# Turning q by a transposing DMA in a pooled attention feeding a GELU layer, with matmuls on zeros and a later load in the first batch

## The chip, the cores and the metric

The kernel runs on one core of a Trainium2 chip. The metric is device time in microseconds (us), the median of several executions. Five engines work side by side, each in the order of its own queue, and wait for each other through semaphores: TensorE (PE; its weight loads are listed as PEld), VectorE (DVE), ScalarE (ACT), GpSimd (POOL) and SyncE (SP). SP, ACT and POOL also issue DMAs. SBUF is the on-chip memory of 128 partitions, PSUM the eight banks that TensorE writes.

## The reference

Inputs are q, k and v of 8 batches, 8 heads, 576 positions and 64 values, and two weight matrices of 512 x 2048 and 2048 x 512, all float32.

```python
k_p = k.reshape(B, H, Sp, 8, D).mean(axis=3)      # Sp = 72
v_p = v.reshape(B, H, Sp, 8, D).mean(axis=3)
scores = scale * np.matmul(q, k_p.transpose(0, 1, 3, 2))
attn = softmax(scores)
attn_out = np.matmul(attn, v_p)                   # (B, H, S, D)
x = attn_out.transpose(0, 2, 1, 3).reshape(B * S, H * D)   # 4608 x 512
g = gelu_tanh(x @ w_in)                           # 4608 x 2048
return g @ w_out                                  # 4608 x 512
```

## The kernel before

The work is written out by hand in one order for every engine; no planner moves it. After a start for batch 0 there are nine stages g = 0 to 8. Stage g runs the two dense layers on rows 512g to 512g + 511 of x, and beside them the attention of batch nb = g + 1, as far as there is one.

A stage has two halves. In the first, TensorE does 64 matmuls of the first layer (`p1_mm`, L266: four per group `fo`, 128 x 512 each), and ACT applies GELU to each group (L272). Between groups the kernel puts work for the next batch, in the lists of `plan`: adding k over its eight pooled positions and v likewise (L135, on VectorE), transposing k (`trans_k`, L162) and q (`trans_q`, L179). A transpose is a TensorE matmul against an identity into a PSUM bank, and VectorE (in batch 0 also ACT) copies the result to `qT` (L184, L186). In the second half TensorE does 64 matmuls of the second layer (`p2_mm`, L275), and at nine fixed places among them the attention of the next batch: scores (`qk`, L196), exponentials (`expo`, L202, ACT), the product with v (`av`, L215; L220 for batch 0), the logarithm and exponential that give the reciprocal of the sum (`norm`, L228 to L233, ACT), and the multiply that writes x transposed, `xT` (`mult`, L241, VectorE). The last multiplies of a batch come behind the last store copy of the stage (L280), and the next stage's first layer reads what they write. TensorE works strictly in its queue's order, so a score matmul that waits holds everything behind it.

In batch 0 the eight score pairs and then eight steps of product, norm and multiply run ahead of stage 0, with 16 first-layer matmuls on 288 columns among the last three steps. In stage 0 the plan has v at groups 1 and 2, k at 7, q at 8 to 11 and the transposes of k at 13.

Loads of k, q (cast to bfloat16) and v of batch g + 2, and the weights, are issued from POOL, and each waits until its buffer is free; two buffers of q alternate. k and v of batch 0 and v of batch 1 are issued from SP at the very start (L76, L96), k's second half from ACT. All stores of the output are issued from SP (L286), from six output buffers.

In `qT` the columns of a head are in the order of positions: `qT[.., h, c, t]`, where q's rows were loaded with 32 groups of 18 positions, c is the group and t one of nine pairs. The two positions of a pair lie on the two halves of the partitions, and `kT` is padded with zeros so that each half can be scored alone.

Of the kernel before, what the change touches and what calls it, by code (L numbers as in the profile page):

```python
# [8 lines left out]
F32 = mybir.dt.float32  # L9
BF16 = mybir.dt.bfloat16  # L10
ALU = mybir.AluOpType
# [7 lines left out]
def kernel(  # L19
# [9 lines left out]
    nc = tc.nc  # L29
    B, H, S, D = q.shape  # L30
    Sp = S // 8
# [6 lines left out]
    TP = T // 2  # L38
    CH = S // 2
# [8 lines left out]
    consts = ctx.enter_context(tc.tile_pool(name="consts", bufs=1))  # L48
    kvp = ctx.enter_context(tc.tile_pool(name="kvp", bufs=2))
    qp = ctx.enter_context(tc.tile_pool(name="qp", bufs=2))  # L50
    bp = ctx.enter_context(tc.tile_pool(name="bp", bufs=2))
# [7 lines left out]
    PS = psp.tile([128, 8, 512], F32, name="PS")  # L59


    vs, qs = {}, {}
# [10 lines left out]
    def load_v(b, eng, h0=0, h1=H):  # L73
        if b not in vs:
            vs[b] = kvp.tile([Sp, H, 512], F32, name="vt")
        eng.dma_start(out=vs[b][:, h0:h1],  # L76
                      in_=v[b, h0:h1].rearrange("h (j l) d -> j h (l d)", l=8))
# [15 lines left out]
    load_k(0, [nc.sync, nc.scalar])  # L93
    load_v(0, nc.sync, 0, 4)
    load_v(0, nc.sync, 4, 8)
    load_v(1, nc.sync)  # L96
    load_q(0, 0, 1)
    load_q(0, 1, 2)
    make_identity(nc, identb)
# [4 lines left out]
    xT = consts.tile([128, KO, N], BF16, name="xT")  # L104

    kTs = [consts.tile([128, 2, H, Sp], BF16, name=f"kT{i}") for i in range(2)]
# [3 lines left out]

    vz = consts.tile([Sp, PR, 2, 2, D], BF16, name="vz")
    ones = consts.tile([Sp, 2, 2, D], BF16, name="ones")
    nc.vector.memset(kts[0][0:64, KR], 0.0)
    nc.vector.memset(kps[0], 0.0)
    nc.vector.memset(kTs[0], 0.0)
# [16 lines left out]
    qTs = {}  # L132
# [22 lines left out]
    def half_bank(bank):  # L155
        return PS[:, bank, :].bitcast(BF16)

    def trans_k(b, bank, odd_eng=None):
        tp = half_bank(bank)[:, 0:(KR + 1) * 128].rearrange("p (r c) -> p r c", c=128)
        kf = kps[b % 2].rearrange("p r d -> p (r d)")  # L160
        for r in range(KR + 1):
            nc.tensor.transpose(out=tp[:, r, :], in_=kf[:, r * D:r * D + 128], identity=identb)  # L162
        tp = tp[0:D]
        n7 = (H - 1) * KH
        for e in range(2):
            copy = nc.scalar.copy if e and odd_eng is nc.scalar else nc.vector.tensor_copy
            o = kTs[b % 2][e * 64:(e + 1) * 64, e]
            copy(out=o[:, 0:H - 1].rearrange("p h (j r) -> p h j r", r=KR),  # L168
                 in_=tp[:, 0:KR, 0:n7].rearrange("p r (h j) -> p h j r", j=KH))
            copy(out=o[:, H - 1, 0:(128 - n7) * KR].rearrange("p (j r) -> p j r", r=KR),  # L170
                 in_=tp[:, 0:KR, n7:128].rearrange("p r j -> p j r"))
            copy(out=o[:, H - 1, (128 - n7) * KR:], in_=tp[:, KR, 64:128])

    def trans_q(b, i, t0, n, bank, eng):
        if b not in qTs:
            qTs[b] = bp.tile([128, 2, 4, 32, TP], BF16, name="qT")
        tp = half_bank(bank)[:, 0:n * 128].rearrange("p (t h c) -> p h c t", h=4, c=32)
        for x in range(n):
            nc.tensor.transpose(out=half_bank(bank)[:, x * 128:(x + 1) * 128],  # L179
                                in_=qs[b][:, i, (t0 + x) * 128:(t0 + x + 1) * 128],  # L180
                                identity=identb)
        o = qTs[b][:, i, :, :, t0:t0 + n]
        if eng is nc.scalar:
            nc.scalar.copy(out=o, in_=tp)  # L184
        else:
            nc.vector.tensor_copy(out=o, in_=tp)  # L186

    QG = [(0, 0, 5), (0, 5, 4), (1, 0, 5), (1, 5, 4)]

# [3 lines left out]
    def qk(b, c, pr, bank):  # L193
        for e in range(2):
            h = 2 * pr + e
            nc.tensor.matmul(out=PS[:Sp, bank + e, :CH], lhsT=kTs[b % 2][:, c, h, :],  # L196
                             rhs=qTs[b][:, h // 4, h % 4].rearrange("p c t -> p (c t)"),
                             start=True, stop=True)

    def expo(b, c, pr, bank):  # L200
# [35 lines left out]
    def mult(b, c, pr, bank):  # L236
        rc = rcs.pop((b, c, pr))
        col = b * S + c * CH
        for x in range(2 if b else 1):
            rows = slice(x * 64, (x + 1) * 64) if b else slice(0, 128)  # L240
            nc.vector.tensor_tensor(out=xT[rows, pr, col:col + CH], in0=PS[rows, bank + x, :CH],  # L241
                                    in1=rc[rows], op=ALU.mult)

    ORDER = [(c, pr) for c in range(2) for pr in range(PR)]

    def act_set(name):
        nc.scalar.preload_act_table_set(name)  # L247
# [45 lines left out]
    for s in k_steps(0):  # L293
        s()

    def scores(b, c, pr, bank):
        qk(b, c, pr, bank)
        expo(b, c, pr, bank)

    trans_q(0, *QG[0], 5, nc.scalar)  # L300
    trans_q(0, *QG[1], 6, nc.scalar)
    trans_k(0, 4, nc.scalar)
    trans_q(0, *QG[2], 5, nc.vector)
    trans_q(0, *QG[3], 6, nc.vector)
    for i, (c, pr) in enumerate(((0, 0), (0, 1), (1, 0), (1, 1), (0, 2), (0, 3), (1, 2), (1, 3))):
        scores(0, c, pr, (2, 0)[i % 2])
    for hf in range(2):
        for s in v_steps(0, hf):
# [4 lines left out]
    for i, (c, pr) in enumerate(ORDER):  # L313
        bank = (4, 6, 0, 2, 4, 6, 4, 6)[i]
        av(0, c, pr, bank)
        norm(0, c, pr, bank)
        mult(0, c, pr, bank)
        for fo, ko in early[:take[i]]:
            p1_mm(0, fo, ko, 0, CH)
        early = early[take[i]:]  # L320


    for g in range(NG):
        nb = g + 1 if g + 1 < B else None
        act_set(GELU_SET)
        if g + 2 < B:
            load_k(g + 2, [nc.gpsimd])
            load_q(g + 2)
            load_v(g + 2, nc.gpsimd)


        side = {fo: [] for fo in range(FO)}
        if nb is not None:
            kk = k_steps(nb)
            v0, v1 = v_steps(nb, 0), v_steps(nb, 1)
            tq = [lambda a=a, i=i: trans_q(nb, *a, 4 + i, nc.vector) for i, a in enumerate(QG)]
            tk = [lambda: trans_k(nb, 4)]
            if g:
                plan = {2: kk[:1], 3: kk[1:], 4: tq[:1], 5: tq[1:2], 6: tq[2:3], 7: tq[3:],
                        9: tk, 10: v0[:1], 11: v0[1:], 12: v1[:1], 13: v1[1:]}  # L340
            else:
                plan = {1: v0, 2: v1, 7: kk, 8: tq[:1], 9: tq[1:2], 10: tq[2:3], 11: tq[3:], 13: tk}
            for fo, what in plan.items():
                side[fo] += what

        if g == 0:
            first = [(fo, ko, CH) for ko in range(KO) for fo in range(4)]
        else:  # L350
            late = 3
            rest = [fo for fo in range(4) if fo != late]
            first = [(fo, ko, 0) for ko in range(2) for fo in rest]
            first += [(late, 0, 0), (late, 1, 0)]
            first += [(fo, ko, 0) for ko in (2, 3) for fo in rest + [late]]
        for fo, ko, c0 in first:
            p1_mm(g, fo, ko, c0)
        for fo in range(FO):
            if fo >= 4:
                for ko in range(KO):  # L360
                    p1_mm(g, fo, ko)
            gelu(g, fo)
            for s in side[fo]:
                s()


        todo = {}

        def at(m, f, *a):
            todo.setdefault(m, []).append((f, a))  # L370

        if nb is not None:
            act_set(EXP_SET)
            pos = (6, 14, 20, 27, 34, 41, 48, 55, 61)
            for i in range(len(ORDER) + 1):
                if i < len(ORDER):
                    at(pos[i], qk, nb, *ORDER[i], 2)
                if i:
                    a = (nb, *ORDER[i - 1], 4 + 2 * ((i - 1) % 2))
                    at(pos[i], av, *a)  # L380
                if i < len(ORDER):
                    at(pos[i], expo, nb, *ORDER[i], 2)
                if i:
                    at(pos[i], norm, *a)
                    at(min(pos[i] + 9, 65), mult, *a)
        seq = [(r, fo) for r in range(4) for fo in range(FO)]
        if g == 0:

            seq[:32] = [(r, 4 * f4 + f) for f4 in range(4) for r in range(2) for f in range(4)]
        for m, (r, fo) in enumerate(seq):  # L390
            for f, a in todo.pop(m, []):
                f(*a)
            p2_mm(g, r, fo)
            if fo == FO - 1:
                store(g, r)
        for m in sorted(todo):
            for f, a in todo[m]:
                f(*a)
# [30 lines left out]
```

The softmax here doesn't subtract the row's maximum and nothing guards it: scores larger than these inputs give would overflow.

## Time and profile before

| | |
|---|---|
| median of 3 executions | 320.53 us (319.16 to 321.37) |
| profiled execution: its own time, and its span | 320.43 us, 318.6 us |
| TensorE busy | 301.7 us, 95% of the span |
| ACT, VectorE, POOL busy | 222.2, 176.3, 29.5 us |
| start to first score matmul of stage 0's attention | 44.73 us |
| stage 2: start, first scores, end | 94.57, 111.23, 127.70 us |
| q transposes (L179) | 144 matmuls, 18 per batch |
| qT copies on VectorE (L186) | 30, 768 ns mean |
| multiplies (L241) | 120, 455 ns mean |

A line of the timeline gives start in us, duration in us, engine, line, operation, output and inputs, and the number of instructions merged into it; in square brackets the idle time of the engine before it and what ended that. Matmul durations overlap, because matmuls are pipelined: the cost of one is read from the distance between starts. "SPq" and "POOL ... DMA" lines are the issuing of a DMA, not its transfer. The row "DMA" gives the mean busy share of the sixteen DMA engines in forty equal slices, in tenths. A group's line gives busy time and mean duration, then the idle time before it.

### The profile page before, as it was taken

The numbers are of one execution on the slowest core, as the hardware profiler recorded it, in microseconds if no ns is written. First come the engines' busy times: TensorE is split into PE (matmuls) and PEld (weight loads), VectorE is DVE, ScalarE is ACT, GpSimd is POOL, SyncE is SP. The second block draws the span as 40 slices with busy tenths as digits, with TensorE's granted clock in tenths as the row PEclk, the third lists the DMA queues.
The fourth block names the chain that finished last, engine by engine and source line by source line (L and its number), as shares of the span: only waits on it lengthen the run. The fifth ranks groups of instructions, "written<-read, shape, count | busy, mean of one in ns | idle before, by whom it ended". The sixth has DMA issues, their size and how long they took to land.

```text
span 318.6 us, 4265 instructions
## 1 busy us (share of the span) xinstructions
PE 301.7 (95%) x1593; PEld 156.7 (49%) x1624; DVE 176.3 (55%) x326; ACT 222.2 (70%) x414; POOL 29.5 (9%) x48
## 2 busy tenths in 40 slices
PE   0699999999999999999999999999999999999995
PEld 0456455454555455445555554555455544444442
DVE  2865836578559845974677467755776560010011
ACT  1585669967897689768985898679867987405500
POOL 8511320021001010101001100000000000000000
PEclk9999999999999999999999999999999999999999
DMA  7999999987722663174418351001200110021021
GB/s 230 262 256 261 227 259 191 248 259 175 175 74 93 165 143 107 38 221 122 125 35 222 90 147 46 0 10 59 66 2 0 66 68 0 18 83 34 0 66 66
DMA packets 17112, 37.50 MB, mean 118 GB/s; under 512 B 2020, under 2 KB 6116, under 8 KB 16196
## 3 DMA queue, kind: packets, MB, share of 16 engines
q0 software_dynamic: 10160, 24.26, 33.3%
q1 hardware_dynamic: 6708, 12.32, 12.0%
q10 hardware_dynamic: 224, 0.66, 0.5%
q8 instruction: 12, 0.20, 0.3%
q14 instruction: 8, 0.07, 0.1%
HBM read 36.70 MB, written 9.44 MB: 145 GB/s over the span
## 4 chain that ended last, share of the span: by engine, by line
PE 82%; DMA 8%; ACT 5%; POOL 3%; issue 1%; DVE 0%; ACTq 0%; POOLq 0%
PE PS L266 36%; PE PS L275 35%; DMA qb<-in_q_dram 8%; PE PS L196 4%; PE PS L215 4%; PE PS L179 2%; ACT e L202 1%; ACT ld L229 1%; ACT ld L228 1%; POOL w_in_b L101 1%; ACT gT L272 1%; PE PS L162 1%; ACT rc L233 1%; POOL kT L120 0%; POOL qb L82 0%
## 5 line engine op out<-in xcount | busy, mean ns | idle before, releaser
L266 PE MATMUL PS<-xT,w_in_b 128*128 128x512 bf16 (+2 forms) x576 | 133.8, 378 | 0.9
L275 PE MATMUL PS<-w_out_b,gT 128*128 128x512 bf16 x561 | 133.9, 379 | 0.5
L272 ACT ACTIVATE gT<-PS 128x512 bf16<-128x512 f32 x144 | 81.7, 602 | 53.3 <-PE PS L266 51.9
L266 PEld LDWEIGHTS <-w_in_b 128*128 128x128 bf16 x592 | 57.2, 99 | 60.1 <-issue 1.5
L275 PEld LDWEIGHTS <-gT 128*128 128x128 bf16 x576 | 56.0, 97 | 56.8 <-issue 0.4
L241 DVE TENSOR_TENSOR xT<-PS,rc 64x288 bf16<-64x288 f32 (+1 forms) x120 | 54.7, 455 | 34.5 <-ACT rc L233 24.7
L280 DVE COPY osb<-PS 128x512 f32<-128x512 f32 x36 | 24.9, 692 | 84.0 <-PE PS L275 84.0
L202 ACT ACTIVATE e<-PS 72x576 bf16<-72x576 f32 x64 | 40.8, 643 | 8.4 <-PE PS L196 7.5
L135 DVE TENSOR_TENSOR vt<-vt 72x1024 f32<-72x1024 f32 (+1 forms) x32 | 30.5, 952 | 0.7
L233 ACT ACTIVATE rc<-ld 128x288 f32<-128x288 f32 x64 | 28.3, 443 | 2.0
L196 PE MATMUL PS<-qT,kT 128*72 128x288 bf16 x128 | 27.6, 304 | 1.2 <-ACT e L202 0.9
L186 DVE COPY qT<-PS 128x640 bf16<-128x640 bf16 (+1 forms) x30 | 22.2, 768 | 3.3 <-PE PS L179 2.9
L228 ACT ACTIVATE ld<-PS 64x288 f32<-64x288 f32 x56 | 22.8, 407 | 1.4
L229 ACT ACTIVATE ld<-PS 64x288 f32<-64x288 f32 x56 | 22.5, 402 | 1.4
L247 ACT ACT_TABLE_LOAD x17 | 21.8, 1283 | 2.0 <-issue 1.8
L215 PE MATMUL PS<-e,vp 72*128 72x288 bf16 x112 | 23.1, 285 | 0.0
L179 PE MATMUL PS<-identb,qb 128*128 128x128 bf16 x144 | 13.9, 231 | 9.6 <-DMA qb<-in_q_dram 9.6
L196 PEld LDWEIGHTS <-kT 128*72 128x72 bf16 x128 | 15.1, 118 | 15.1 <-issue 2.1
L135 DVE TENSOR_TENSOR kt<-kt 128x1280 f32<-128x1280 f32 (+1 forms) x16 | 18.5, 1158 | 5.3 <-DMA kt<-in_k_dram 4.8
L179 PEld LDWEIGHTS <-qb 128*128 128x128 bf16 x144 | 11.2, 104 | 16.5 <-DMA qb<-in_q_dram 10.1
L168 DVE COPY kT<-PS 64x504 bf16<-64x504 bf16 x15 | 10.1, 675 | 9.4 <-PE PS L162 9.3
L215 PEld LDWEIGHTS <-vp 72*128 72x128 bf16 x112 | 11.0, 98 | 3.3
(40 smaller groups left out, 77.4 us busy)
## 6 DMA issues: line engine op xcount, KB each, us to landing
kt<-in_k_dram POOLq DMA_DIRECT2D x7, 1024.0 KB, 10.6
vt<-in_v_dram POOLq DMA_DIRECT2D x6, 1152.0 KB, 9.8
out_dram<-osb SPq DMA_DIRECT2D x24, 256.0 KB, 2.1
qb<-in_q_dram POOLq DMA_DIRECT2D x7, 576.0 KB, 10.9
w_in_b<-in_moe_w_in_dram POOLq DMA_DIRECT2D x4, 512.0 KB, 20.4
w_out_b<-in_moe_w_out_dram POOLq DMA_DIRECT2D x4, 512.0 KB, 22.2
out_dram<-osb SPq DMA_DIRECT2D x8, 192.0 KB, 2.2
vt<-in_v_dram SPq DMA_DIRECT2D x2, 576.0 KB
```

The lines of the kernel that those rows point to most:

```text
L135: nc.vector.tensor_tensor(out=o, in0=a, in1=b, op=ALU.add)
L179: nc.tensor.transpose(out=half_bank(bank)[:, x * 128:(x + 1) * 128], in_=qs[b][:, i, (t0 + x) * 128:(t0 + x + 1) * 128], identity=identb)
L196: nc.tensor.matmul(out=PS[:Sp, bank + e, :CH], lhsT=kTs[b % 2][:, c, h, :], rhs=qTs[b][:, h // 4, h % 4].rearrange("p c t -> p (c t)"), st ...
L202: nc.scalar.activation(out=e, in_=PS[:Sp, bank:bank + 2, :CH], func=ACT.Exp, scale=1.0 / 64.0)
L215: nc.tensor.matmul(out=PS[:, bank + x, :CH], lhsT=flat(vps[b % 2][:, pr, x]), rhs=e[:, x, :], start=True, stop=True)
L228: nc.scalar.activation(out=ld[0:64], in_=PS[64:128, bank, :CH], func=ACT.Ln)
L229: nc.scalar.activation(out=ld[64:128], in_=PS[0:64, bank + 1, :CH], func=ACT.Ln)
L233: nc.scalar.activation(out=rc, in_=ld, func=ACT.Exp, scale=-1.0)
L241: nc.vector.tensor_tensor(out=xT[rows, pr, col:col + CH], in0=PS[rows, bank + x, :CH], in1=rc[rows], op=ALU.mult)
L266: nc.tensor.matmul(out=PS[:, h_bank(g, fo), c0:c1], lhsT=w_in_b[:, ko, fo * 128:(fo + 1) * 128], rhs=xT[:, ko, r0 + c0:r0 + c1], start=(ko ...
L272: nc.scalar.activation(out=gTs[g][:, fo, :], in_=PS[:, h_bank(g, fo), :], func=ACT.Gelu_apprx_tanh)
L275: nc.tensor.matmul(out=PS[:, o_bank(g, r), :], lhsT=gTs[g][:, fo, r * 128:(r + 1) * 128], rhs=w_out_b[:, fo, :], start=(fo == 0), stop=(fo ...
```

## The change

Four things are changed together.

1. For batches 1 to 7, q is turned by one transposing DMA per batch, issued from SP at the head of the stage (`trans_q_dma`): 18 blocks of 128 x 128 from `qb` to `qT`, both in SBUF. The `plan` loses its q entries and its other entries move. Batch 0 keeps its transposes on TensorE.
2. `qT` is laid out as `[128, 2, 9, 128]`, pair t outermost and then head and group. `qk` therefore reads nine runs of 32 columns, and the scores' columns are in the order (t, c). `mult` puts them back in order of position: it writes `xT` with a step of nine elements.
3. `spin(n)` issues n matmuls of 128 x 512 on a tile of zeros into bank 7: sixteen ahead of the first q transposes, four ahead of k's, two ahead of the first scores, one ahead of each later score pair of batch 0. Nothing reads their results.
4. The load of batch 1's v is no longer issued at the start. It is issued from SP after the fourth multiply of batch 0; a one-column memset on VectorE behind that multiply is what it waits for.

```diff
-    load_v(1, nc.sync)
     load_q(0, 0, 1)
...
+    idle = consts.tile([128, 512], BF16, name="idle")
+    nc.vector.memset(idle, 0.0)
...
     def trans_q(b, i, t0, n, bank, eng):
         if b not in qTs:
-            qTs[b] = bp.tile([128, 2, 4, 32, TP], BF16, name="qT")
-        tp = half_bank(bank)[:, 0:n * 128].rearrange("p (t h c) -> p h c t", h=4, c=32)
+            qTs[b] = bp.tile([128, 2, TP, 128], BF16, name="qT")
+        tp = half_bank(bank)[:, 0:n * 128].rearrange("p (t c) -> p t c", c=128)
...
-        o = qTs[b][:, i, :, :, t0:t0 + n]
+        o = qTs[b][:, i, t0:t0 + n]
...
+    def trans_q_dma(b):
+        qTs[b] = bp.tile([128, 2, TP, 128], BF16, name="qT")
+        nc.sync.dma_start_transpose(out=qTs[b].rearrange("p i t c -> p (i t) c"),
+                                    in_=qs[b].rearrange("p i c -> p (i c)"))
...
-            nc.tensor.matmul(out=PS[:Sp, bank + e, :CH], lhsT=kTs[b % 2][:, c, h, :],
-                             rhs=qTs[b][:, h // 4, h % 4].rearrange("p c t -> p (c t)"),
+            nc.tensor.matmul(out=PS[:Sp, bank + e, :CH].rearrange("j (t p) -> j t p", p=32),
+                             lhsT=kTs[b % 2][:, c, h, :],
+                             rhs=qTs[b][:, h // 4, :, h % 4 * 32:h % 4 * 32 + 32],
                              start=True, stop=True)
...
-            nc.vector.tensor_tensor(out=xT[rows, pr, col:col + CH], in0=PS[rows, bank + x, :CH],
-                                    in1=rc[rows], op=ALU.mult)
+            nc.vector.tensor_tensor(
+                out=xT[rows, pr, col:col + CH].rearrange("p (c t) -> p t c", t=TP),
+                in0=PS[rows, bank + x, :CH].rearrange("p (t c) -> p t c", t=TP),
+                in1=rc[rows].rearrange("p (t c) -> p t c", t=TP), op=ALU.mult)
...
+    def spin(n):
+        for _ in range(n):
+            nc.tensor.matmul(out=PS[:, 7, :], lhsT=idle[:, 0:128], rhs=idle, start=True, stop=True)
...
+    spin(16)
     trans_q(0, *QG[0], 5, nc.scalar)
     trans_q(0, *QG[1], 6, nc.scalar)
+    spin(4)
     trans_k(0, 4, nc.scalar)
     trans_q(0, *QG[2], 5, nc.vector)
     trans_q(0, *QG[3], 6, nc.vector)
+    spin(2)
     for i, (c, pr) in enumerate(((0, 0), (0, 1), (1, 0), (1, 1), (0, 2), (0, 3), (1, 2), (1, 3))):
+        if i:
+            spin(1)
         scores(0, c, pr, (2, 0)[i % 2])
...
         mult(0, c, pr, bank)
+        if i == 3:
+            vs[1] = kvp.tile([Sp, H, 512], F32, name="vt")
+            nc.vector.memset(vs[1][:, 0, 0:1], 0.0)
+            load_v(1, nc.sync)
...
-            tq = [lambda a=a, i=i: trans_q(nb, *a, 4 + i, nc.vector) for i, a in enumerate(QG)]
+            trans_q_dma(nb)
...
-                plan = {2: kk[:1], 3: kk[1:], 4: tq[:1], 5: tq[1:2], 6: tq[2:3], 7: tq[3:],
-                        9: tk, 10: v0[:1], 11: v0[1:], 12: v1[:1], 13: v1[1:]}
+                plan = {2: kk[:1], 3: kk[1:], 7: v0[:1], 8: v0[1:], 9: tk, 11: v1[:1], 12: v1[1:]}
             else:
-                plan = {1: v0, 2: v1, 7: kk, 8: tq[:1], 9: tq[1:2], 10: tq[2:3], 11: tq[3:], 13: tk}
+                plan = {1: v0, 2: v1, 7: kk, 12: tk}
```

## The prediction

> **What bounds the kernel now.** I read the page first: busy shares, the chain that ended last, the slices.
>
> ```profile
> PE 301.7 (95%) x1593; PEld 156.7 (49%) x1624; DVE 176.3 (55%) x326; ACT 222.2 (70%) x414; POOL 29.5 (9%) x48
> ...
> DMA  7999999987722663174418351001200110021021
> ...
> PE 82%; DMA 8%; ACT 5%; POOL 3%; issue 1%; DVE 0%; ACTq 0%; POOLq 0%
> ```
>
> TensorE is the bound: 95% busy, 82% of the chain. The DMA row is full only in the first eight slices (64 us). So after the start every TensorE instruction removed is time, as long as nothing new ends late. Then the timeline of stage 2 (94.57 to 127.70 us), whose pattern the stages 1 to 6 repeat:
>
> ```profile
> 94.77 0.69 DVE L280 COPY osb<-PS 128x512 f32<-128x512 f32 x1 [1.49 <-PE PS L275]
> ...
> 95.49 28.77 SPq L286 DMA_DIRECT2D out_dram<-osb  x4
> 95.49 1.88 DVE L241 TENSOR_TENSOR xT<-PS,rc 64x288 bf16<-64x288 f32 x4
> ...
> 99.15 0.44 PE L179 MATMUL PS<-identb,qb 128*128 128x128 bf16 x5
> ...
> 99.43 1.03 PE L266 MATMUL PS<-xT,w_in_b 128*128 128x512 bf16 x4
> ...
> 100.30 0.39 PE L179 MATMUL PS<-identb,qb 128*128 128x128 bf16 x4
> ...
> 100.52 1.03 PE L266 MATMUL PS<-xT,w_in_b 128*128 128x512 bf16 x4
> ...
> 103.21 0.72 POOL L82 DMA_DIRECT2D qb<-in_q_dram  x1 [1.50 <-PE PS L179]
> ...
> 111.23 0.41 PE L196 MATMUL PS<-qT,kT 128*72 128x288 bf16 x2
> ```
>
> Five transposes move the next matmul by 99.43 - 99.15 = 0.28 us, four by 0.22: 56 ns each, with no idle around them. At 103.21 POOL already loads the q of batch 5, so the q that stage 2 turns (batch 3) has lain there for a stage. The four multiplies behind the last store copy end at 97.37. Last the start:
>
> ```profile
> 18.71 0.68 PE L220 MATMUL PS<-e,ones 72*128 72x288 bf16 x2
> ...
> 19.19 0.68 PE L220 MATMUL PS<-e,vz 72*128 72x288 bf16 x2
> ...
> 28.89 1.93 DVE L135 TENSOR_TENSOR vt<-vt 72x1024 f32<-72x1024 f32 x2
> ...
> 33.40 0.55 POOL L71 DMA_DIRECT2D kt<-in_k_dram  x1 [3.59 <-DMA kt<-in_k_dram]
> ...
> 36.10 0.45 PE L179 MATMUL PS<-identb,qb 128*128 128x128 bf16 x5 [0.73 <-DMA qb<-in_q_dram]
> ...
> 44.73 0.41 PE L196 MATMUL PS<-qT,kT 128*72 128x288 bf16 x2
> ```
>
> Two 288-column matmuls take 0.48 us here, 0.24 each; in stage 2 the score pair at 111.23 moves its follower (111.47) by 0.24, 0.12 each. The first batch runs at half rate. The k of batch 1 lands at about 33.4, its q at 36.1.
>
> **What the skill says.** (1) "TensorE: Matmul & The Clock Gate", Part 1: an array that was idle passes half the clock until about 3.4 us of activity. The trace agrees (0.24 against 0.12), though its granted-clock row reads full throughout. (2) "DMA: Bandwidth & Descriptors", Latency and other measured facts: 261 GB/s for a DMA transpose. (3) "VectorE: DVE Perf Modes", The three transpose paths: 1309 ns for one 128x128 tile by DMA. No transposing DMA runs here, so the two are my bounds. (4) "SBUF — State Buffer", Door 1: lines of 16 bytes, with a penalty for accesses that each hit a new line. No row here writes with such a step.
>
> **The change, part by part.** *Transposes off TensorE.* Batches 2 to 7 lose 18 x 56 ns = 1.0 us in each of stages 1 to 6: 6.0 us, all on the path. VectorE loses four copies of some 0.77 us a stage; it waits for TensorE anyway, worth nothing.
>
> *The transposing DMA.* It stands on SP behind the last store of the stage before (95.49) and ahead of this stage's stores; q and the buffer have long been free. The first scores want qT at 111.23 - 1.0 = 110.2, so it has 14.3 us (from 95.9, SP's issue of the store off). Queued behind it on SP: stores, the first wanted 20 us later with six output buffers, so no cost. Queued behind the scores on TensorE: every second-layer matmul, so lateness is paid in full. Size 128 x 2304 x 2 B = 0.59 MB. Lower bound 0.59 MB / 261 GB/s = 2.3 us plus the 2.1 us in which 256 KB stores land: 4.4. Upper bound 18 x 1.309 = 23.6 us, one tile after another. I take 5 to 7, an estimate, since sixteen DMA engines share the tiles: hidden in stages 1 to 6. POOL's q loads now wait for this DMA instead of TensorE, with the v load behind; both are a stage early, no cost.
>
> *Layout.* Score matmuls read 32 adjacent columns at a time (64 bytes, whole lines), price 0. Multiplies write xT with a step of 18 bytes. From below 0: the old qT copy wrote runs of 4 and 5 elements at that pitch at about one element per cycle (0.72 us for 512, 0.83 for 640). From above, half rate: 288 elements at 0.96 GHz, 0.30 us more each. I take 0. The batch-0 qT copies become contiguous: 0 to 0.3 us each, in work that waits elsewhere, 0.
>
> *Zero matmuls.* Sixteen before q arrives: cold 512 columns are 0.43 us each, 6.8 us at most, between 1.9 and 8.9: in idle time. The other 13 (0.22 us warm) lie where TensorE waited for kp (0.86 us) or for the exponentials (0.59 us of ACT per pair of 0.24 us of matmuls). They cost nothing, and if TensorE stays warm the eight steps of the first batch's second half are paced by ACT: 0.40 + 0.44 = 0.84 us plus hand-over, say 0.9, instead of 0.96, and the 16 early first-layer matmuls (0.24 each) vanish in the gaps. Last multiply at about 25.4 instead of 28.97: 3.6 us gained here. If it cools again, nothing.
>
> *What eats that.* v of batch 1 is issued after the fourth multiply, at about 21.5, on SP, beside POOL's stream in saturated DMA. By 36.1 the DMAs had read about 11.3 MB (k, q, v of batches 0 and 1 at 1.18 MB each, w_in 4.2): 320 GB/s. At half of that, 1.18 MB takes 7.4 us; it lands at 29 to 31. VectorE then needs 4.8 us for v (28.89 to 33.7 before) and 2.85 for k (33.72 to 36.6): kp at 37 to 38.7. TensorE reaches k's transposes (after twelve groups) at about 34.4 and stalls; 0.28 for them, 2.6 for three groups, 1.3 for six second-layer matmuls: first scores at 41.5 to 43. The q of batch 1 still lands at 36.1, total bytes being equal; its turn, in saturated DMA, ends at 42 to 44. Against 44.73 that is 0.7 to 3; the idle of 3 us may also cool the array. I take 1.0.
>
> *Sum.* 6.0 + 1.0 = 7.0. The profiled execution took 320.43 (span 318.6, 1.8 around it), 0.1 below the median of 320.53: 320.43 - 7.0 = 313.4.
>
> **Rivals.** *A, the DMA is late (slower).* Place: the first scores of each stage. Point: stages 1 to 6 lose from 14.3 us on, stage 0 from about 6.5. At 23.6: 6 x 9.3 = 56, and stage 0 (36.1 + 23.6 against 43) 16.7: 313.4 + 73 = 386. Slower than before by 1% from about 15 us. For: the single-tile price, saturated DMA up to 64 us. Against: the 261 GB/s, idle DMA later (45% share in stage 2).
>
> *B, strided multiplies.* Four follow the last store copy and gate the first layer; TensorE waits some 0.1 us there already. At 0.30 more each the second ends 0.6 later and the fourth 1.2 later, about 1.2 us a stage, 7 stages: 8.4, so 321.8; at half that 317.6. For: the line rule. Against: the copies named above.
>
> *C, the start goes wrong.* The held v delays k by 3 to 4 us more, or the first turn takes 10 us in the queue: stage 0 loses 3, total 320.4 - 6 + 3 = 317.4.
>
> **How the numbers follow.** Forecast 0.58 (309.5 to 316), B 0.17 (317 to 323), C 0.07 (316 to 319), A 0.18. The range 309 to 323 leaves A out. One per cent, about what a measurement here can tell from no change, is 3.2 us: faster is below 317.3. Faster: the forecast and a third of B and C, 0.63. Same: most of B and C, a little of A: 0.17. Slower: 0.20.
>
> **What would show it.** Right: 18 transposes left on TensorE, stages 1 to 6 of 31.9 us instead of 32.9, qT landing before the first scores without a wait, matmuls of 0.12 us in the first batch, a wait for kp in stage 0. Wrong: TensorE waiting for qT in every stage (A); multiplies of 0.75 us instead of 0.455 and a wait for xT at the stage's start (B); first scores of stage 0 after 45 us (C).

## The result and the profile after

The changed kernel takes 428.93 us (median of 4, 427.99 to 431.87) against 320.95 us for the kernel before (median of 4): 1.339 times as long, 95% interval 1.331 to 1.348. The forecast was 313.4, the range 309 to 323. The profiled execution took 429.48 us, span 427.6, 109.0 more than before.

The page of the changed kernel (busy shares, the granted TensorE clock and the DMA share in forty slices, the chain that ended last, the costliest group, and the transposing DMA's median from issue to landing):

```profile
PE 324.9 (76%) x1498; PEld 153.1 (36%) x1527; DVE 270.6 (63%) x300; ACT 222.4 (52%) x414; POOL 29.5 (7%) x48
...
PEclk9969667996999899988999899989998999899999
DMA  8999998224530464146513561220114010002102
...
PE 40%; DVE 32%; DMA 13%; issue 7%; ACT 5%; POOL 2%; POOLq 0%
...
L248 DVE TENSOR_TENSOR xT<-PS,rc 64x288 bf16<-64x288 f32 (+1 forms) x120 | 169.9, 1433 | 30.7 <-ACT rc L240 27.7
...
qT<-qb SPq DMA_TRANSPOSE x7, 5.0
```

TensorE has fallen from 82% of the chain to 40%, and VectorE, absent from it before, holds 32%. The multiply takes 1433 ns instead of 455; 120 of them are 169.9 us instead of 54.7. The transposing DMA lands in 5.0 us in the median. Next the timeline around the head of stage 2, which began at 138.21 us, as stages 1 to 6 repeat it:

```profile
138.41 0.69 DVE L289 COPY osb<-PS 128x512 f32<-128x512 f32 x1 [1.02 <-PE PS L284]
...
139.13 5.73 DVE L248 TENSOR_TENSOR xT<-PS,rc 64x288 bf16<-64x288 f32 x4
139.58 2.84 SPq L191 DMA_TRANSPOSE qT<-qb  x1
142.03 1.02 PE L275 MATMUL PS<-xT,w_in_b 128*128 128x512 bf16 x4 [1.94 <-DVE xT L248]
...
144.91 7.80 PE L275 MATMUL PS<-xT,w_in_b 128*128 128x512 bf16 x28 [1.86 <-DVE xT L248]
...
158.01 1.46 PE L284 MATMUL PS<-w_out_b,gT 128*128 128x512 bf16 x6
...
159.30 0.41 PE L202 MATMUL PS<-qT,kT 128*72 128x288 bf16 x2
...
166.67 0.28 PE L222 MATMUL PS<-e,vp 72*128 72x288 bf16 x1 [1.07 <-DVE xT L248]
```

And two lines of stage 2 of the kernel before, for comparison:

```profile
104.75 5.34 PE L266 MATMUL PS<-xT,w_in_b 128*128 128x512 bf16 x24
109.93 1.46 PE L275 MATMUL PS<-w_out_b,gT 128*128 128x512 bf16 x6
```

The four multiplies behind the store copy take 5.73 us instead of 1.88, and the first layer waits for them twice (1.94 and 1.86 us). The 28 matmuls behind the second wait take 7.80 us, where at the pace of the kernel before (24 in 5.34) they would take 6.2: they start at half rate. The product with v waits for each earlier multiply to free its bank (1.07 us here, 43 such waits and 43.1 us in the whole table of waits). The first scores at 159.30 wait for nothing: the turn was issued at 139.58 and takes some 5 us. The start, in order of time:

```profile
17.12 0.41 PE L227 MATMUL PS<-e,vz 72*128 72x288 bf16 x2
17.37 0.41 PE L227 MATMUL PS<-e,ones 72*128 72x288 bf16 x2
...
31.99 10.93 SPq L191 DMA_TRANSPOSE qT<-qb  x1
...
38.43 1.94 DVE L136 TENSOR_TENSOR vt<-vt 72x1024 f32<-72x1024 f32 x2 [8.36 <-DMA vt<-in_v_dram]
...
46.28 0.69 PE L163 MATMUL PS<-identb,kp 128*128 128x128 bf16 x5 [7.75 <-DVE kp L136]
```

```profile
64.55 0.67 PE L202 MATMUL PS<-qT,kT 128*72 128x288 bf16 x2 [12.54 <-DMA qT<-qb]
```

The first batch runs at full rate (a pair each 0.25 us). Then stage 0 loses it all: v of batch 1 lands at 38.4, TensorE waits 7.75 us for the pooled k (`kp`), and 12.54 us more for the q of batch 1, whose turn was issued at 31.99 and landed 32.4 us later, at 64.4.

The sum: stage 1 begins at 92.14 instead of 61.45 (+30.7). The six stages to the start of stage 7 take 363.34 - 92.14 = 271.2 instead of 259.40 - 61.45 = 197.95 (+73.3, 12.2 each). From there to the end, with the wait for the last multiplies at the head of stage 7, it is the remaining 5. That is 109.

### The profile page after: what moved, and what is told of

Its sections match the earlier page's. It is cut to its first block, busy times and chain, and to the rows that moved or that the text cites. A ratio compares the mean times of both kernels' runs of the same rounds, so it can differ in the third digit from the quotient of the medians.

```text
span 427.6 us, 4057 instructions
## 1 busy us (share of the span) xinstructions
PE 324.9 (76%) x1498; PEld 153.1 (36%) x1527; DVE 270.6 (63%) x300; ACT 222.4 (52%) x414; POOL 29.5 (7%) x48
## 3 DMA queue, kind: packets, MB, share of 16 engines
q0 software_dynamic: 10160, 24.26, 25.4%
## 4 chain that ended last, share of the span: by engine, by line
PE 40%; DVE 32%; DMA 13%; issue 7%; ACT 5%; POOL 2%; POOLq 0%
DVE xT L248 29%; PE PS L275 24%; PE PS L284 13%; DMA qT<-qb 8%; DMA qb<-in_q_dram 5%; DVE osb L289 3%; ACT ld L235 2%; ACT e L209 1%; ACT rc L240 1%; ACT ld L236 1%; PE PS L202 1%; PE PS L222 1%; POOL w_in_b L100 1%; PE PS L163 0%; POOL kT L121 0%
## 5 line engine op out<-in xcount | busy, mean ns | idle before, releaser
L248 DVE TENSOR_TENSOR xT<-PS,rc 64x288 bf16<-64x288 f32 (+1 forms) x120 | 169.9, 1433 | 30.7 <-ACT rc L240 27.7
L275 PE MATMUL PS<-xT,w_in_b 128*128 128x512 bf16 (+2 forms) x579 | 144.5, 407 | 26.5 <-DVE xT L248 24.8
L284 PE MATMUL PS<-w_out_b,gT 128*128 128x512 bf16 x561 | 135.4, 382 | 0.7
L275 PEld LDWEIGHTS <-w_in_b 128*128 128x128 bf16 x592 | 61.5, 105 | 104.5 <-issue 35.0
L222 PE MATMUL PS<-e,vp 72*128 72x288 bf16 x112 | 29.9, 288 | 45.0 <-DVE xT L248 43.1
L202 PE MATMUL PS<-qT,kT 128*72 128x288 bf16 x128 | 26.7, 291 | 13.5 <-DMA qT<-qb 12.5
L70 POOL DMA_DIRECT2D kt<-in_k_dram x7 | 4.0, 574 | 155.2 <-DVE kp L136 153.1
L308 PE MATMUL PS<-idle 128*128 128x512 bf16 x28 | 9.3, 455 | 1.2 <-DVE idle L113 1.2
L163 PE MATMUL PS<-identb,kp 128*128 128x128 bf16 x40 | 3.8, 230 | 8.3 <-DVE kp L136 8.3
```

Of the source, the lines that this page charges most:

```text
L202: nc.tensor.matmul(out=PS[:Sp, bank + e, :CH].rearrange("j (t p) -> j t p", p=32), lhsT=kTs[b % 2][:, c, h, :], rhs=qTs[b][:, h // 4, :, h ...
L222: nc.tensor.matmul(out=PS[:, bank + x, :CH], lhsT=flat(vps[b % 2][:, pr, x]), rhs=e[:, x, :], start=True, stop=True)
L248: nc.vector.tensor_tensor(out=xT[rows, pr, col:col + CH].rearrange("p (c t) -> p t c", t=TP), in0=PS[rows, bank + x, :CH].rearrange("p (t ...
L275: nc.tensor.matmul(out=PS[:, h_bank(g, fo), c0:c1], lhsT=w_in_b[:, ko, fo * 128:(fo + 1) * 128], rhs=xT[:, ko, r0 + c0:r0 + c1], start=(ko ...
L284: nc.tensor.matmul(out=PS[:, o_bank(g, r), :], lhsT=gTs[g][:, fo, r * 128:(r + 1) * 128], rhs=w_out_b[:, fo, :], start=(fo == 0), stop=(fo ...
```

## The experiments

Theory 1: the multiply's stepped write is the main cost. Theory 2, rival A of the prediction: the transposing DMA is. A ratio is the measured time over that of the kernel before, with its 95% interval. The comparisons are within groups of runs on one chip, whose kernel before took 319.49, 321.02 and 320.61 us.

**The multiply without a step.**

```diff
 # the changed kernel
-out=xT[..].rearrange("p (c t) -> p t c", t=TP), in0=PS[..].rearrange("p (t c) -> p t c", t=TP), ...
+out=xT[rows, pr, col:col + CH], in0=PS[rows, bank + x, :CH], in1=rc[rows]
```

> The changed kernel, but the multiply writes xT without a step, in the order in which it reads (t, c); this leaves out putting the rows of x back in the order of positions. Theory 1, the stepped write is the main cause: multiplies back to 0.45 us, stages 1 to 6 at about 31.9 us, and only stage 0's wait for the transposed q remains (first scores about 64 us instead of 44.7): 325 to 340 us. Theory 2, the transposing DMA is the main cause (rival A in every stage): stays above 400 us.

Measured 339.77 us, ratio 1.063 (1.058 to 1.067). The multiply's group, and from the timeline the first scores of stage 0:

```profile
L248 DVE TENSOR_TENSOR xT<-PS,rc 64x288 bf16<-64x288 f32 (+1 forms) x120 | 54.7, 455 | 51.4 <-PE PS L222 26.2 <-ACT rc L240 22.9
```

```profile
67.73 0.67 PE L202 MATMUL PS<-qT,kT 128*72 128x288 bf16 x2 [15.03 <-DMA qT<-qb]
```

Taking the step away gives back 88 of the 108 us. What is left is stage 0: stage 1 begins at 86.47 instead of 61.45, after waits of 11.6 us for the pooled k and 15.0 for q. Stages 1 to 6 take 32.1 and 31.9 us, each 1.0 less than in the kernel before: the transposes that are gone, and no price for the scores' reads of the new `qT`.

**The step alone, in the kernel before.**

```diff
 # the kernel before
-out=xT[rows, pr, col:col + CH], in0=PS[rows, bank + x, :CH], in1=rc[rows]
+out=xT[..].rearrange("p (c t) -> p t c", t=TP), in0=PS[..].rearrange("p (t c) -> p t c", t=TP), ...
```

> The kernel before, with only the multiply's write changed to a step of nine elements (this puts the rows of x out of the order of positions). Theory 1: multiplies at about 1.43 us, steady stages at about 45 us instead of 32.9, so 390 to 415 us. Theory 2: multiplies alone cost little, under 330 us.

Measured 409.62 us, ratio 1.281 (1.276 to 1.287), with no transposing DMA in the program. Its multiply's group:

```profile
L241 DVE TENSOR_TENSOR xT<-PS,rc 64x288 bf16<-64x288 f32 (+1 forms) x120 | 169.9, 1433 | 14.2 <-ACT rc L233 5.7 <-PE PS L215 5.5
```

The step alone costs 90 us, the rest of the change without it 20; together 110 against 108 measured. Theory 1 holds for the main part.

**What a step costs.**

```diff
+n = (9, 2, 3, 4, 6, 8, 16, 32)[b]     # the step in batch b
-out=xT[rows, pr, col:col + CH], ...
+out=xT[..].rearrange("p (c t) -> p t c", t=n), in0=PS[..].rearrange("p (t c) -> p t c", t=n), ...
```

> The kernel before, with the multiply's write stepped differently in each batch: 9 elements of two bytes in batch 0, then 2, 3, 4, 6, 8, 16, 32 in batches 1 to 7 (rows of x out of order). If the cost comes with each new 16-byte line: 0.45 us at steps 2 and 3, full 1.43 us from step 8 on, little more at 16 and 32. If it comes with every write that does not fill its word: 1.43 us from step 2 on. If it grows with distance: still rising between 9 and 32. Total between 330 and 410 us.

Measured 363.11 us (one run). The multiply's group in the windows of batches 1 to 7, that is at steps of 2, 3, 4, 6, 8, 16 and 32 elements of two bytes, mean duration in ns behind the comma (the last three windows are 188 to 217, 230 to 263 and 275 to 308 us):

```profile
L242 DVE TENSOR_TENSOR xT<-PS,rc 64x288 bf16<-64x288 f32 x16 | 7.7, 479 | 6.6 <-PE PS L215 5.5 <-ACT rc L233 0.7
L242 DVE TENSOR_TENSOR xT<-PS,rc 64x288 bf16<-64x288 f32 x16 | 10.2, 640 | 2.3 <-ACT rc L233 2.0
L242 DVE TENSOR_TENSOR xT<-PS,rc 64x288 bf16<-64x288 f32 x16 | 12.8, 799 | 1.3 <-ACT rc L233 0.9
L242 DVE TENSOR_TENSOR xT<-PS,rc 64x288 bf16<-64x288 f32 x16 | 17.9, 1116 | 1.1 <-ACT rc L233 0.6
L242 DVE TENSOR_TENSOR xT<-PS,rc 64x288 bf16<-64x288 f32 x16 | 22.9, 1433 | 1.0 <-ACT rc L233 0.6
L242 DVE TENSOR_TENSOR xT<-PS,rc 64x288 bf16<-64x288 f32 x16 | 22.2, 1386 | 1.1 <-ACT rc L233 0.6
L242 DVE TENSOR_TENSOR xT<-PS,rc 64x288 bf16<-64x288 f32 x16 | 22.5, 1404 | 1.1 <-ACT rc L233 0.6
```

The cost rises up to a step of 8 elements, 16 bytes, and is nearly flat from there. That is what a price per line of 16 bytes gives. From step 3 on it rises in a straight line: a step of n up to 8 enters 36 n lines, and (799 - 640) / 36, (1116 - 799) / 72 and (1433 - 1116) / 72 are all 4.4 ns a line. For an element the kernel before gives 1.03 ns: its adds of v (L135) take 1216 ns for 1024 elements and 687 for 512, which leaves some 160 ns for the instruction. So an estimate for a multiply is 160 ns plus the larger of 300 ns, for 288 elements, and 4.4 ns for each line entered. It gives 460 without a step (measured 455), 477, 635, 794, 1110 and 1427 at 2, 3, 4, 6 and 8 (479, 640, 799, 1116, 1433). Where multiplies of the first batch follow each other without a wait in the changed kernel, they start 1.27 us apart, which is 288 x 4.4 ns. Neither "every write that doesn't fill a word" nor "distance" fits. The expectation had seen the line rule but put step 3 at 0.45; it is 0.64, because below 4.3 writes per line (4.4 ns over 1.03 ns an element) the line is the limit already. Only two-byte elements were tried, so a line of 16 bytes is not told apart from a run of 8 elements.

**The step on the other side.**

```diff
 # the changed kernel
-out=xT[..].rearrange("p (c t) -> p t c", t=TP), in0=PS[..].rearrange("p (t c) -> p t c", t=TP), ...
+out=xT[..].rearrange("p (c t) -> p c t", t=TP), in0=PS[..].rearrange("p (t c) -> p c t", t=TP), ...
```

> The changed kernel, with the multiply walking its 288 columns in the order of xT: the write has no step, the two reads (PSUM and the float32 reciprocal in SBUF) step by 32 elements, 128 bytes. Computes the full result. If only stepped writes cost: multiplies 0.45 to 0.5 us and the total of the unstepped variant, 325 to 340 us. If a step costs on the read side too: multiplies over 1 us and over 390 us.

Measured 341.44 us, ratio 1.068 (1.063 to 1.073).

```profile
L248 DVE TENSOR_TENSOR xT<-PS,rc 64x288 bf16<-64x288 f32 (+1 forms) x120 | 77.3, 644 | 41.1 <-PE PS L222 25.3 <-ACT rc L240 12.8
```

The same reordering costs 0.19 us on the read side and 0.98 on the write side. At most 0.05 had been expected; which of the two reads causes it was not tried.

**Why the first turn is late.** The landing times told two cases apart: 32.4 us in stage 0, beside POOL's loads, and 5 later. The loads behind the turn were held back:

```diff
 # the variant without a step; v of batch 1 at the start
             trans_q_dma(nb)
+            if g == 0:
+                nc.gpsimd.tensor_copy(out=guard, in_=qTs[nb][:, 0, 0, 0:1])
+                # and only now the four loads of w_out
             # and only now the loads of k, q, v of batch g + 2
```

> The unstepped variant with v of batch 1 at the start and with the loads of w_out and of k, q, v of batch 2 issued only once the turned q of batch 1 has landed, so that the transposing DMA of batch 1 runs beside almost no other traffic (rows of x out of order; w_out comes late, so the total says nothing). If its 32 to 34 us in stage 0 come from sharing the DMA engines with POOL's stream of loads: lands in 5 to 8 us. If the first transposing DMA is slow by itself: stays near 30 us.

From its timelines of SP and of POOL, the issue, and the first instruction that had waited for the landing:

```profile
35.32 2.85 SPq L191 DMA_TRANSPOSE qT<-qb  x1
```

```profile
40.03 0.18 POOL L351 COPY guard<-qT 128x1 bf16<-128x1 bf16 x1 [28.56 <-DMA qT<-qb]
```

It landed in 4.7 us. (The total, 338.44 us in one run, says nothing, because w_out comes late.) The batch is the same and only its neighbours are gone, so the loads from POOL beside it are the cause. The held loads then ran in stage 1, and there the next turn was issued at 67.62 with SP held for 15.12 us instead of 2.8.

The packets of the queues hint at the manner: number, MB, share of 16 engines. First while the changed kernel's first turn ran (35.9 to 64 us; q0 is POOL's loads, q1 almost only the turn), then beside another late turn, that of batch 2 in the first repair below (65.3 to 92.2 us), last for the turn alone in the run with the loads held (36.6 to 39.6 us):

```profile
q0 software_dynamic: 2064, 4.63, 82.8%
q1 hardware_dynamic: 2378, 0.65, 32.3%
```

```profile
q1 hardware_dynamic: 2597, 1.04, 60.4%
q0 software_dynamic: 558, 2.09, 37.9%
```

```profile
q1 hardware_dynamic: 2336, 0.59, 104.6%
```

In the first the loads passed about one packet for each of the turn's, as if the two took turns. In the second they passed one for four or five, and the turn still took 27 us. Share x 16 engines x window over packets gives 61 and 100 ns for a packet of q1 there, and 21 ns alone. So the turn's own packets are slowed too, and taking turns one for one is not the whole manner, which stays open.

**The held v, in the changed program and alone.**

```diff
 # the variant without a step
     load_v(0, nc.sync, 4, 8)
+    load_v(1, nc.sync)
...
-        if i == 3:
-            vs[1] = kvp.tile(...); nc.vector.memset(...); load_v(1, nc.sync)
```

```diff
 # the kernel before
-    load_v(1, nc.sync)
...
+        if i == 3:
+            vs[1] = kvp.tile(...); nc.vector.memset(...); load_v(1, nc.sync)
```

> The unstepped variant with v of batch 1 loaded at the start instead of being held. If in stage 0 the late turn of q decides and the hold is masked by it: the pooled k is ready by 37 us, but the first scores still wait for the turned q until 64 to 70 us, total 335 to 343, about as with the hold (339.8). If the hold decides: first scores below 55 us, total below 328.

> The kernel before with only the v of batch 1 held back to the fourth multiply. If that hold is a cost of its own: v lands near 38 us, the pooled k of batch 1 some 8 us later than now, TensorE waits for it, 3 to 6 us in all: 323 to 327 us. If it is hidden: 319 to 321.

The first: 342.55 us, ratio 1.068 (1.060 to 1.076). The pooled k is ready at 36.2, yet the first scores, in its timeline, wait:

```profile
70.01 0.66 PE L203 MATMUL PS<-qT,kT 128*72 128x288 bf16 x2 [27.91 <-DMA qT<-qb]
```

So without the hold the variant is no faster (1.063 with it): the hold's cost is hidden, because q is later still. The second, the hold alone in the kernel before: 327.68 us, ratio 1.023 (1.015 to 1.031), 6.7 us. VectorE waits 10.7 us for v; k's sums, and behind them the copies of q that free the bank for k's transposes, queue behind it. From its timeline:

```profile
45.84 0.69 PE L161 MATMUL PS<-identb,kp 128*128 128x128 bf16 x5 [7.89 <-DVE qT L185]
```

There TensorE stands still for 7.89 us. These are two parts of one change, and the cost of the one hides that of the other.

**The matmuls on zeros alone.**

```diff
 # the kernel before
+    spin(16) ... spin(4) ... spin(2) ... spin(1)   # at the changed kernel's places
```

> The kernel before with only the 29 matmuls on zeros. First batch at full clock (0.12 us per 288 columns instead of 0.24), its last multiply some 3 us earlier; the q of batch 1 still lands at 36 us, so at most 0.7 to 1 us of that reaches the end: 319 to 320.5 us. If the clock gain carried through: 317.

Measured 321.82 us (20 executions) against 321.02 (23): ratio 1.003 (1.0005 to 1.005). No gain, if anything a loss. Its timeline shows why:

```profile
34.83 0.71 PE L181 MATMUL PS<-identb,qb 128*128 128x128 bf16 x5 [4.61 <-DMA qb<-in_q_dram]
...
37.46 1.85 PE L268 MATMUL PS<-xT,w_in_b 128*128 128x512 bf16 x4
39.15 0.44 PE L181 MATMUL PS<-identb,qb 128*128 128x128 bf16 x5
39.43 1.03 PE L268 MATMUL PS<-xT,w_in_b 128*128 128x512 bf16 x4
40.29 0.39 PE L181 MATMUL PS<-identb,qb 128*128 128x128 bf16 x4
```

TensorE is earlier, waits 4.61 us for the q of batch 1 where it waited 0.73, and comes out of the wait at half rate (four matmuls move the next instruction by 39.15 - 37.46 = 1.69 us, and once warm by 40.29 - 39.43 = 0.86). Its first scores start at 45.54, 0.8 us later than in the kernel before.

**Repairs.** The reordering moves to the exponential on ACT, which reads PSUM with a step and writes without one; v is back at the start; q of batch 1, or of batches 1 and 2, stays on TensorE.

```diff
-nc.scalar.activation(out=e, in_=PS[:Sp, bank:bank + 2, :CH], func=ACT.Exp, ...)
+nc.scalar.activation(out=e.rearrange("j x (c t) -> j x c t", t=TP),
+                     in_=PS[:Sp, bank:bank + 2, :CH].rearrange("j x (t c) -> j x c t", t=TP), ...)
```

> The changed kernel with three repairs: the exponentials read the scores in order of position (stepped PSUM read, plain write), so the multiply is the plain one; v of batch 1 is loaded at the start again; q of batch 1 is turned on TensorE as before. Full result. If the transposing DMA is slow only beside the saturated loads and these are over by stage 1: stages 1 to 6 give 1.0 us each from batch 2 on, 312 to 316 us. If batch 2's turn (issued about 61 us, loads running to 72) still takes 30 us: a wait of some 15 us in stage 1, about 330. If the stepped PSUM read slows ACT (exponential 0.65 us now): another 1 us a stage for each 0.2 us.

> As the kernel with three repairs, but q of batches 1 and 2 both on TensorE, the DMA from batch 3 on. Removes any wait in stage 1; costs 1.0 us more on TensorE. 313 to 317 us in either theory; better than the variant with batch 2 by DMA only if that waits in stage 1.

Measured 333.04 us (ratio 1.039; 1.027 to 1.050) with batch 1 alone on TensorE and 317.28 (0.990; 0.978 to 1.001), not clear of no change, with both. In the first, batch 2's turn meets the loads of stage 1, as its timeline says:

```profile
92.72 0.67 PE L203 MATMUL PS<-qT,kT 128*72 128x288 bf16 x2 [13.08 <-DMA qT<-qb]
```

The exponential takes 644 ns, as in the changed kernel, and 643 in the kernel before: ACT's stepped read of PSUM costs nothing here. There are two more, without the zero matmuls. The first keeps batches 1 and 2 on TensorE; the second keeps batch 1 alone there, and holds POOL's loads until the stage's turn has landed.

> The repaired kernel with q of batches 1 and 2 on TensorE, without the matmuls on zeros. If these only bring TensorE earlier to the same wait for q of batch 1 and let it cool there: equal or better than with them, 314.5 to 317 us. If they helped: 318 to 319.

> As the kernel without matmuls on zeros, but batch 2 by DMA too, with POOL's loads of batch g + 2 held until the stage's turned q has landed (a one-column copy on GpSimd waits for it), so that no transposing DMA meets the stream of loads. If sharing is the cause: batch 2's turn lands in about 5 us instead of 30, no wait in stage 1, 313.5 to 316 us. If not: a wait of 13 us in stage 1, about 330.

Measured 315.28 us (ratio 0.985; 0.978 to 0.992) and 316.27 (0.985; 0.977 to 0.992). Both are faster than the kernel before, by some 1.5%, and neither measurably faster than the other. In the second, batch 2's turn was issued at 64.75, from the timelines of SP and POOL, and had landed at

```profile
69.51 0.68 POOL L343 COPY guard<-qT 128x1 bf16<-128x1 bf16 x1 [31.78 <-DMA qT<-qb]
```

4.8 us later, without a wait in stage 1. That is what the loads as the cause predict.

## Why the prediction was wrong

The step that failed is *Layout*: it took half rate, 0.30 us more for each multiply, as the bound from above, and 0 as the price. The cost is 0.98 us. The rule of 16-byte lines in the Trainium skill's "SBUF — State Buffer", Door 1, had been quoted a paragraph earlier, and lines are what the measured steps fit. But the page gives no price, and its statement that two hits per line are enough is not borne out: step 4, two per line, took 799 ns. Half rate was taken for a bound without a reason: nothing in the trace limited a line to the time of two elements, and it takes that of 4.3.

The reason given from below was wrong as well. The old `qT` copy did write at an 18-byte pitch, in runs of 4 and 5 elements: it entered 128 x 18 / 16 = 144 lines for 512 or 640 elements. The multiply enters 288 for 288. At 4.4 ns a line the copy's 144 lines would be 0.63 us, close to what its elements take at 1.03 ns each (0.53 and 0.66), so it could not show the price. Pitch was compared where lines per instruction should have been. Nor was the copy free: the contiguous ones of the changed kernel's first batch took 406 and 473 ns on VectorE, where the old ones took 716 and 820. How much of that is the write was not tried, since the old copy also read PSUM with a step; and 716 is less than 0.63 us and the multiply's 160 ns together, so the price does not carry over exactly.

- *Rival B* named the right place, the four multiplies behind the last store copy. It was priced at 1.2 us a stage; stages lost 12.2 more than before, 13.2 against the forecast. In stage 2 the half up to the second layer took 19.80 us instead of 15.36 - 1.0, 5.4 more: 3.8 of waits, and 1.6 because the matmuls behind them started at half rate. B left out the other half, 25.44 us instead of 17.77: there slower multiplies hold the banks of the product with v, and eight pairs of 2.86 us make 22.9 us of VectorE.
- *The transposing DMA* in stages 1 to 6: "5 to 7", hidden. Right: 5.0 us, no wait from stage 1 on. Rival A, the slower ending, was right on the sign, but by luck: its mechanism was wrong in every stage but 0.
- *Its turn in saturated DMA* "ends at 42 to 44": wrong, 64.4. It was given 6 to 8 us, only 1 more than a turn with nothing beside it, and its 32.4 us lie above even the upper bound of 23.6. Alone it took 4.7 us from issue to landing, close to the lower bound of 4.4: the Trainium skill's 1309 ns for one tile ("VectorE: DVE Perf Modes", The three transpose paths) does not add up over 18 tiles here.
- *The held v*: to land at 29 to 31, landed at 38.4; the pooled k at 37 to 38.7, was at 46. The share of one half was too much: 1.18 MB from 23.8 to 38.4 are 81 GB/s, a quarter of what the prediction reckoned (11.3 MB in 36.1 us, 313 GB/s rather than its 320). The q of batch 1, "still at 36.1", came at 32.0 in return. Alone this costs 6.7 us; the forecast counted it inside a gain of 1.0.
- *Transposes off TensorE*: 1.0 us a stage, right. In the repaired kernel with the DMA from batch 3 on and the zero matmuls, stages 3 and 6 begin at 129.30 and 225.12 us, 31.9 us a stage, and in the kernel before at 127.70 and 226.54, 32.9.
- *Zero matmuls*: "cost nothing" and full rate in the first batch, right (0.12 us per 288 columns; without a step the last multiply starts at 24.55 and ends at 25.0, forecast 25.4). That little of it would reach the end was also right: alone, nothing did.
- *The chances* do not add up: the forecast's 0.58 and a third of B's and C's 0.24 make 0.66 for faster, not 0.63, and 0.20 for slower is more than A's 0.18.

## What to carry to other kernels

Before a layout change is priced, count how many 16-byte lines each instruction writes, not only its elements: on VectorE each new line cost 4.4 ns here, so a bf16 write is free of it only from about five neighbours per line on. Put a reordering on a read side: on VectorE's reads it cost 0.19 us instead of 0.98, on ACT's read of PSUM nothing. A DMA of many small packets that landed in 5 us with little beside it took 32 beside a stream of loads, so price it by what runs beside it, and hold the stream if it must be on time.

## What the runs showed of the hardware

- A stepped bf16 write on VectorE, 288 elements that take 455 ns without a step: 479, 640, 799, 1116, 1433 ns at steps of 2, 3, 4, 6, 8 elements, then 1386 at 16 and 1404 at 32.
- The granted-clock row reads full at the start of the kernel before, though matmuls run at half rate there (0.24 us per 288 columns, 0.12 later). In the changed kernel it does show the slow stretch of stage 0 with its waits (0.76 between 32 and 64.5 us).
- A contiguous copy of the batch-0 q from PSUM to SBUF in bf16 took 473 ns for 640 elements on VectorE, where the copy with a step on both sides had taken 820.
- The transposing DMA's packets of 256 bytes took 21 ns each alone, and 61 and 100 ns beside loads.
